# A fused RWKV and token-mixing kernel: V used as it is loaded, on 64-row tiles, instead of being brought into another order

## The chip, the cores and the metric

The kernel runs on one core of a Trainium2 chip. TensorE (PE) does the matrix products, VectorE (DVE), ScalarE (ACT) and GpSimd (POOL) the elementwise work, and SyncE (SP) issues most of the DMAs. The metric is the device time of one execution in microseconds (us); lower is better. Where the text says "the span", it means the time from the first to the last instruction in the one execution that the hardware profiler recorded.

## The reference

Two layers follow each other. The first is a recurrence over 768 time steps, for 4 batches and 8 heads with 48 values each; the second mixes the tokens of a batch.

```python
for t in range(S):                                   # S = 768
    cur = np.einsum('bhd,bhe->bhde', u[None] * kt, vt)
    y[:, :, t] = np.einsum('bhd,bhde->bhe', rt, state + cur)
    state = wt[:, :, :, None] * state + np.einsum('bhd,bhe->bhde', kt, vt)
...
x = y.transpose(0, 2, 1, 3).reshape(B, S, H * D)     # H * D = 384
wq, wk = x @ w_q, x @ w_k                            # d_hyper = 64
W_tok = scale * np.einsum('bsd,btd->bst', wq, wk)
mixed = np.einsum('bst,btd->bsd', W_tok, x)
out = np.maximum(mixed, 0.0) @ w_out
```

`w` is a decay between 0.8 and 0.95, and `u` is a bonus that only the present step's key and value get. Inputs and output are float32.

## The kernel before

The recurrence is computed in chunks of 128 steps. Two chunks make a *unit*; a batch has three units and the kernel twelve. For a unit, four loads bring w, k, r and v (384 KB each). One partition of a load holds two neighbouring time steps of all heads, so that a row in DRAM is 384 bytes long; partitions 0 to 63 then hold the first chunk and 64 to 127 the second. The steps of a unit, by the names that the profile shows, are these:

- `lw`: logarithm of w (ACT). `cw`: its running sum by a product with a triangular matrix CM, whose columns bring the even and the odd time steps apart. `ep` and `en`: exp of plus and minus that sum (ACT).
- `kT`, `rT`: k and r (cast to bfloat16 as `k16`, `r16`) are transposed on PE; `ks` is a copy of k transposed, `qT` the product of r and k. `RT` is r times `ep`, `KT` is k times `en`.
- `A`: KT against RT, the scores of a chunk, two heads at a time on the two halves of the array's rows; `AM`: the scores under the causal mask US (DVE, L713).
- `v16`, `vp`, `VB`: v is cast, brought by PE into the even-then-odd order that all else has (`vp`, by a permutation matrix PM or by identity blocks), and copied out of PSUM. In the last batch the two loads `vw` bring V in that order directly, with 64 partitions and 192-byte rows each.
- `dps`, `dd`: the bonus per head and step; `Vd`: VB times that bonus (POOL, L693).
- `kb`, `kd`: KT transposed back; `sn`, `SB`: the new state, from kd and VB, plus the old state through the scaled identity IDU, times the decay (DVE, L772).
- `yi`, `ya`: old state times RT, and AM times VB, added in PSUM. `X` is that sum times a factor per time step (`gx`) plus Vd, in one DVE instruction (scalar_tensor_tensor, L831). The decay is shifted by an amount that grows with the time step, and gx, gv and gk take it out again.
- `xt`, `XT`: X transposed. `qk`, `QK`: the products with w_q (twice side by side, 128 columns) and w_k, and their copy.

When a batch's three units are done, `T` adds up K times X over the six chunks (two halves of PSUM's partitions get the even and the odd chunks), `mx` multiplies with Q, `MX` is the relu, `fp` the product with w_out, `os` its copy out of PSUM and `st` the store. In the last unit most steps are done chunk by chunk.

PE addresses its array as one tile of 128 rows by 128 columns, or as two of 64 by 128, or two of 128 by 64, or four of 64 by 64. Tiles that differ run side by side. In the profile's rows "128\*128", "64\*128", "48\*128" (48 rows of a 64-row tile), "128\*64" and "64\*64" stand for that. Every matmul is recorded in the helper `mm`, so all have one line, L275.

The order of the work is written out: a `Plan` holds every step, with the engines that may do it, and the lists RANK (the place of each step on its engine) and ALT (which engine or which form it takes) fix one order. `Plan.order` only merges the engines' lists. Buffers are rings (`RINGS`: four for each load, four for `os`), and PSUM's eight banks are handed out in the plan's order. Loads and stores are all on SP's queue but for two: a load waits there until its ring has a free buffer, and everything behind it waits too. `Z` products are fillers without a use in the result.

Of the kernel before, what the change touches and what calls it, by code (L numbers as in the profile page):

```python
# [10 lines left out]
F32 = mybir.dt.float32  # L11
# [22 lines left out]
class Plan:  # L34
# [15 lines left out]
    def add(self, key, engs, fn, after=(), buf=None, reads=(), lag=None, mode=0, behind=None,  # L50
            part=None):
        opts = {}
        for e, x in engs.items():
            x = x if isinstance(x, tuple) else (x, mode, None)
            own = self.AFTER[e.upper()] if lag is None else lag
            over = self.OVER.get(e, 0) if fn is not None else 0
            opts[e] = (e.upper(), x[0] - over, own + over, x[1], x[2])
# [135 lines left out]
    0, 0, 0, 0, 2, 7, 4, 3, 5, 6, 17, 0, 0, 18, 3, 1, 4, 2, 0, 0, 0, 1, 0, 0, 2, 0, 0, 4, 0, 0,  # L193
    1, 2, 1, 4, 3, 4, 3, 6, 5, 5, 8, 8, 13, 10, 9, 12, 11, 5, 17, 9, 26, 19, 9, 11, 18, 15, 22,
    16, 12, 14, 16, 8, 23, 18, 30, 22, 42, 44, 43, 45, 30, 74, 27, 87, 34, 3, 0, 0, 5, 0, 0, 6,
    0, 0, 7, 0, 0, 7, 6, 7, 21, 10, 11, 24, 25, 17, 23, 21, 20, 8, 27, 13, 37, 17, 14, 41, 27,
    32, 24, 31, 15, 38, 26, 56, 32, 52, 55, 64, 68, 37, 82, 32, 90, 36, 9, 0, 0, 8, 0, 0, 11, 0,
    0, 10, 0, 0, 14, 12, 12, 35, 18, 16, 36, 46, 25, 28, 29, 13, 10, 47, 20, 62, 34, 15, 53, 31,
    59, 33, 54, 21, 63, 35, 69, 71, 73, 72, 39, 84, 35, 92, 38, 98, 41, 103, 43, 110, 47, 49, 0,
    0, 115, 49, 127, 55, 50, 0, 0, 126, 68, 139, 60, 51, 0, 0, 12, 0, 0, 14, 0, 0, 15, 0, 0, 16,  # L200
    0, 0, 19, 22, 17, 60, 24, 25, 66, 76, 36, 41, 40, 38, 16, 78, 29, 81, 31, 20, 80, 43, 86,
    46, 79, 42, 83, 44, 96, 50, 89, 95, 91, 97, 51, 106, 44, 124, 52, 13, 0, 0, 18, 0, 0, 19, 0,
    0, 22, 0, 0, 23, 30, 33, 70, 26, 28, 85, 88, 45, 47, 48, 19, 21, 100, 42, 108, 57, 26, 104,
    54, 93, 49, 99, 52, 107, 58, 113, 60, 118, 120, 123, 122, 66, 141, 61, 154, 67, 21, 0, 0,
    20, 0, 0, 23, 0, 0, 24, 0, 0, 37, 22, 23, 94, 40, 39, 101, 105, 53, 56, 55, 25, 24, 109, 46,
    111, 59, 29, 116, 62, 114, 61, 112, 48, 125, 65, 128, 129, 131, 133, 70, 146, 64, 160, 70,
    170, 75, 174, 78, 186, 83, 48, 0, 0, 177, 79, 209, 98, 52, 0, 0, 189, 86, 219, 101, 53, 0,
# [28 lines left out]
def kernel(  # L236
# [63 lines left out]
    if not WHOLE:  # L300
        del RINGS["vw"]
# [726 lines left out]
```

## Time and profile before

| | |
|---|---|
| time, median of 3 runs | 105.08 us (104.53, 105.49, 105.08) |
| span of the profiled execution | 101.6 us; the page gives no other time of it, so 3.5 us of the median lie around the span |
| granted PE clock | 0.992 over the span (0.85 from 95 us on, 1.00 before) |
| PE busy | 90.9 us, 1,881 matmuls and as many weight loads |
| DVE, ACT, POOL busy | 84.2, 80.6 and 64.9 us |
| DMA | 24.66 MB, mean 243 GB/s; queue q1 takes 87.3% of 16 engines |
| last load issued, landed | 70.9 us, 75.8 us |
| last product `fp` | from 94.2 to 97.3 us; the last store is issued at 97.8 and has landed by 100.4 |

A matmul's row gives the time from its start to a modelled end, some 180 to 330 ns, while the next matmul starts much earlier. How long a step holds PE is therefore read from the start of its first matmul to the start of the next step's.

### The profile page before, as it was taken

Reading aid. Unit: us, or ns where it says so; the run is one execution under the profiler, and the core shown is the slowest. Engines: PE = TensorE matmul, PEld = TensorE weight load, DVE = VectorE, ACT = ScalarE, POOL = GpSimd, SP = SyncE. Lnnn points to the kernel's source line nnn. Section 1 sums busy time; section 2 is a strip of 40 time slices with the busy share of each in tenths; the row PEclk is TensorE's granted clock in tenths of the full one; section 3 lists DMA queues with packets and bytes.
Section 4 is the critical chain, followed back from the end, with each engine's and each line's share of the span. In section 5 each row is a group of like instructions: output and inputs, shape, how many; then the busy total and the mean of one; then the engine's idle time right before and its main releaser. Section 6 shows DMA issues by size and latency. Waiting matters only on the chain.

```text
span 101.6 us, 4422 instructions
## 1 busy us (share of the span) xinstructions
PE 90.9 (90%) x1881; PEld 65.5 (64%) x1881; DVE 84.2 (83%) x146; ACT 80.6 (79%) x123; POOL 64.9 (64%) x75
## 2 busy tenths in 40 slices
PE   5968897999989989999899999998999999999920
PEld 2344674757748766677586985776888677967600
DVE  5089998799889969979999999999989999894500
ACT  6364697959699789998999999999987946666940
POOL 6474662991895699889968999896899540000000
PEclk9999999999999999999999999999999999999996
DMA  1999999999999999999999799999999132103793
GB/s 38 310 324 325 325 321 248 296 308 259 321 275 274 304 248 305 300 320 240 275 302 279 198 256 286 167 196 186 211 371 350 39 155 105 56 3 155 284 365 125
DMA packets 56403, 24.66 MB, mean 243 GB/s; under 512 B 54080, under 2 KB 55232, under 8 KB 56384
## 3 DMA queue, kind: packets, MB, share of 16 engines
q1 hardware_dynamic: 56224, 24.19, 87.3%
q8 instruction: 14, 0.23, 0.9%
q10 hardware_dynamic: 160, 0.20, 0.5%
q14 instruction: 5, 0.04, 0.1%
HBM read 19.66 MB, written 4.72 MB: 240 GB/s over the span
## 4 chain that ended last, share of the span: by engine, by line
PE 57%; DVE 10%; SPq 9%; ACT 7%; DMA 6%; POOL 3%; issue 3%; DVEq 0%; ACTq 0%; POOLq 0%
PE PS L275 57%; SPq L328 9%; DMA wg<-in_w_dram 6%; DVE AM L713 5%; ACT lw L500 2%; POOL Vd L693 1%; DVE ks L426 1%; DVE qT L599 1%; ACT os L420 1%; POOL r L511 1%; ACT QK L420 1%; ACT ep L551 1%; DVE X L831 1%; DVE SB L772 1%; ACT XT L420 1%
## 5 line engine op out<-in xcount | busy, mean ns | idle before, releaser
L713 DVE TENSOR_TENSOR AM<-PS,US 128x1024 bf16<-128x1024 f32 x24 | 28.9, 1218 | 0.8 <-PE PS L275 0.8
L693 POOL TENSOR_TENSOR Vd<-VB,dd 128x768 bf16<-128x768 bf16 (+1 forms) x14 | 18.3, 1316 | 5.0 <-DVE dd L426 3.8
L624 POOL TENSOR_TENSOR KT<-ks,en 128x1024 bf16<-128x1024 bf16 x8 | 17.1, 2132 | 5.1 <-DVE ks L426 4.8
L551 ACT ACTIVATE ep<-PS 128x1024 bf16<-128x1024 f32 (+1 forms) x14 | 12.9, 927 | 1.3 <-PE PS L275 0.8
L275 PE MATMUL PS<-wo,MX 128*128 128x384 bf16 x72 | 13.3, 326 | 0.2 <-DVE SB L772 0.2
L556 ACT ACTIVATE en<-PS 128x1024 bf16<-128x1024 f32 (+1 forms) x14 | 12.5, 903 | 0.9 <-PE PS L275 0.9
L275 PEld LDWEIGHTS <-KT 48*128 48x128 bf16 (+1 forms) x304 | 10.0, 94 | 4.7 <-issue 2.7
L275 PE MATMUL PS<-Z 128*128 128x512 bf16 x36 | 11.9, 435 | 1.0 <-DVE Z L342 1.0
L831 DVE SCALAR_TENSOR_TENSOR X<-PS,gx,Vd 128x768 bf16<-128x768 f32 (+1 forms) x13 | 12.4, 950 | 0.3 <-PE PS L275 0.2
L500 ACT ACTIVATE lw<-wg 128x768 bf16<-128x768 f32 x12 | 10.2, 849 | 2.6 <-DMA wg<-in_w_dram 2.6
L420 ACT COPY os<-PS 128x768 f32<-128x768 f32 (+1 forms) x14 | 9.3, 663 | 2.7 <-PE PS L275 2.6
L511 POOL CAST r<-rg 128x768 bf16<-128x768 f32 x11 | 9.6, 872 | 0.4 <-DMA rg<-in_r_dram 0.4
L275 PE MATMUL PS<-RT,KT 48*128 48x128 bf16 x192 | 9.6, 218 | 0.0
L647 POOL CAST v<-vg 128x768 bf16<-128x768 f32 x9 | 7.4, 825 | 3.5 <-DMA vg<-in_v_dram 3.5
L275 PEld LDWEIGHTS <-MX 128*128 128x128 bf16 x72 | 6.5, 97 | 4.3 <-issue 0.9
L420 ACT COPY XT<-PS 128x768 bf16<-128x768 bf16 (+1 forms) x11 | 8.5, 771 | 0.5 <-ACT en L556 0.2
L614 DVE TENSOR_TENSOR RT<-PS,ep 128x1024 bf16<-128x1024 bf16 (+1 forms) x14 | 8.4, 606 | 0.3 <-PE PS L275 0.3
L599 DVE TENSOR_TENSOR qT<-PS,ks 128x1024 bf16<-128x1024 bf16 x12 | 8.2, 683 | 0.4 <-PE PS L275 0.4
L275 PE MATMUL PS<-SB,RT 48*128 48x48 bf16 x160 | 6.7, 182 | 1.9 <-ACT QK L420 0.2
L772 DVE TENSOR_TENSOR SB<-PS,ep 128x192 bf16<-128x192 f32 x20 | 7.0, 351 | 1.4 <-PE PS L275 1.4
L275 PE MATMUL PS<-CM,lw 64*128 64x128 bf16 x192 | 7.5, 217 | 0.8 <-ACT lw L500 0.8
L275 PE MATMUL PS<-VB,AM 128*128 128x48 bf16 x192 | 8.2, 184 | 0.0
(89 smaller groups left out, 192.4 us busy)
## 6 DMA issues: line engine op xcount, KB each, us to landing
wg<-in_w_dram SPq DMA_DIRECT2D x12, 384.0 KB, 5.1
kg<-in_k_dram SPq DMA_DIRECT2D x12, 384.0 KB, 5.5
rg<-in_r_dram SPq DMA_DIRECT2D x12, 384.0 KB, 5.6
vg<-in_v_dram SPq DMA_DIRECT2D x9, 384.0 KB, 5.6
out_dram<-os SPq DMA_DIRECT2D x9, 384.0 KB, 2.4
vw<-in_v_dram SPq DMA_DIRECT2D x4, 288.0 KB, 6.6
out_dram<-os SPq DMA_DIRECT2D x5, 192.0 KB, 2.4
wof<-in_moe_w_out_dram SPq DMA_DIRECT2D x1, 576.0 KB, 4.9
```

Of the source, the lines that this page charges most:

```text
L275: return nc.tensor.matmul(o, l, rr, start=start, stop=stop, skip_group_check=True, is_transpose=trans)
L328: nc.sync.dma_start(out=view(tl, 0, [[D2, H], [1, D2]]), in_=ap[b, :, ds(i * U, U)].rearrange("h (p j) d -> p h (j d)", j=2))
L420: nc.scalar.copy(o, i)
L500: nc.scalar.activation(view(lw.tile, 0, [[64, H], [512, 2], [1, D]]), view(g["wg"].tile, 0, [[D2, H], [D, 2], [1, D]]), ACT.Ln, bias=0.0, ...
L511: op(view(o.tile, 0, [[64, H], [512, 2], [1, D]]), view(g[src].tile, 0, [[D2, H], [D, 2], [1, D]]))
L551: nc.scalar.activation(view(ep.tile, cs[0] * NP * EW + 66, [[EW, NP * len(cs)], [-65, 2], [1, 64]]), at(cw)[:, ds(cs[0] * 512, w_)], ACT.E ...
L556: nc.scalar.activation(en.tile[:, ds(cs[0] * 512, w_)], at(cw)[:, ds(cs[0] * 512, w_)], ACT.Exp, bias=0.0, scale=-1.0)
L599: lambda e: nc.vector.tensor_tensor(view(qT.tile, 0, [[512, 2], [1, 512]]), turned(second), view(ks.tile, 0, [[512, 2], [1, 512]]), ALU.mult),
L624: x.tensor_tensor(o, view(ks.tile, cs[0] * 512, dims), y, ALU.mult)
L693: nc.gpsimd.tensor_tensor(Vd.tile[:, cols], VB.tile[:, cols], view(dd.tile, cs[0] * H, [[1, len(cs) * H], [0, D]]), ALU.mult)
L713: AMs[c] = add(("AM", n, c), {"D": 1221}, lambda e, c=c, A=A: nc.vector.tensor_tensor(view(AM[c].tile, 0, [[C, 8], [1, C]]), view(at(A), 0 ...
L831: nc.vector.scalar_tensor_tensor(view(X.tile, (2 * i + c0) * DM, [[DM, nc_], [1, DM]]), view(at(y), 0, [[512, nc_], [1, DM]]), gx, view(Vd ...
```

## The change

V stays in the order in which it was loaded: partitions 0 to 63 hold the first chunk, two neighbouring time steps side by side (index j). Whatever meets V is turned to suit it.

- `vp`, `VB`, PM and the `vw` loads go; the last batch loads V like the others (12 `vg` loads of 128 partitions).
- `A` is cut by j instead of by chunk: its outputs are 64 partitions (one chunk's even or odd keys). `ya` contracts over 64 rows, for two chunks, two j and two halves of the output: 64 matmuls per unit on 64x64 tiles where there were 16. `kb` and `sn` are cut alike; the old state is added by `so`, two matmuls of 128x64 per chunk.
- `Vd` is v16 times the bonus; it is added in PSUM by four products with identity blocks (`yd`), and `X` becomes a plain copy that ACT or DVE can do.
- The decay's shift is one constant (`up`, `dn` as biases of `ep` and `en`); gx, gv and gk go, and US is a 128x256 mask without factors, made on POOL.
- Q is computed once, chunk 0 on partitions 0 to 63 and chunk 1 on 64 to 127; QK has 256 columns where it had 384. `T` adds all six chunks on both halves (12 matmuls where there were 6), and `mx` takes 64 rows per chunk.
- `cw`, `kT`, `rT`, `xt`, `mx` and `fp` may be cut in two halves of output partitions (`mms`), which puts them on 64x64 or 128x64 tiles.
- `os` has 7 buffers (4 before), `v16` 3 (2 before); RANK and ALT are new.

The counts, from the two programs' instruction lists: PE has 3,941 matmuls (1,881 before), 3,000 of them on 64x64 tiles (12 before). The tile shape changes 103 times along PE's list (99 before). Z products are 22 (36 before). PE's queue drains go from 16 to 3. Leaving out waits, branches, table loads and DMAs, DVE has 144 instructions (146 before), ACT 111 (122) and POOL 65 (75). SP starts with k, w, r, k, v, w, r, w where it started with w, k, r, w, v, k, r, v, k, w; one store of 384 KB stands ahead of the last four loads, where all stores stood behind all loads.

```diff
+    def mms(split, o, l, rr, **kw):
+        if not split:
+            return mm(o, l, rr, **kw)
+        for half in range(2):
+            mm(o[ds(half * 64, 64)], l[:, ds(half * 64, 64)], rr, **kw)
...
-        wg=(4, HW, F32), rg=(4, HW, F32), kg=(4, HW, F32), vg=(4, HW, F32), os=(4, 2 * DM, F32),
...
+        wg=(4, HW, F32), rg=(4, HW, F32), kg=(4, HW, F32), vg=(4, HW, F32), os=(7, 2 * DM, F32),
...
-                vps = add(("vp", n), {"E": (330, 1, None), "e": (185, 3, None)}, f_vp,
-                          [v16s, wts["p"]], vp, [v16])
-                VBs = add(("VB", n), copies(2 * DM), lambda e: copy(
-                    e, view(VB.tile, 0, [[DM, 2], [1, DM]]),
-                    view(at(vp), 0, [[512, 2], [1, DM]])), [vps], VB, [vp])
...
+        Vds = add(("Vd", n), {"P": 1477, "D": 900}, lambda e: (
+            nc.vector if e == "D" else nc.gpsimd).tensor_tensor(
+            Vd.tile, v16.tile, view(dd.tile, 0, [[1, 2 * H], [0, D]]), ALU.mult),
+            [v16s, dds], Vd, [v16, dd])
...
-                        mm(x[:, ds(hh * 512 + hp * C, C)],
-                           KT.tile[ds(hh * 64, D), ds((c * NP + hp) * C, C)],
-                           RT.tile[ds(hh * 64, D), ds((c * NP + hp) * C, C)])
+                    for c in range(2):
+                        for hh in range(2):
+                            x = (c * NP + hp) * C
+                            mm(at(A)[ds(c * 64, 64), ds(hh * 512 + hp * C, C)],
+                               KT.tile[ds(hh * 64, D), ds(x + j * 64, 64)],
+                               RT.tile[ds(hh * 64, D), ds(x, C)])
...
-                        mm(x[:, ds(hp * D, D)],
-                           kd.tile[:, ds(64 + (c * H + h) * 128 - 64 * hh, 128)],
-                           VB.tile[:, ds(c * DM + h * D, D)],
...
+                            mm(at(sn)[ds(hh * 64, 64), ds(c * 512 + hp * D, D)],
+                               kd.tile[rows, ds(hh * 512 + (j * NP + hp) * 64, 64)],
+                               v16.tile[rows, ds(j * DM + (2 * hp + hh) * D, D)],
+                               start=(j == 0 and hp == 0))
...
-                if not first:
-                    nc.tensor.drain()
                 for hp in range(NP):
                     for c, hh in side:
-                        mm(of(c, 2 * hp + hh), RT.tile[ds(hh * 64, D), ds((c * NP + hp) * C, C)],
+                        mms(first, of(c, 2 * hp + hh),
+                            RT.tile[ds(hh * 64, D), ds((c * NP + hp) * C, C)],
...
-                    mm(of(c, h), AM[c].tile[:, ds(hh * 512 + hp * C, C)],
-                       VB.tile[:, ds(c * DM + h * D, D)],
+                    for c in range(2):
+                        rows = ds(c * 64, 64)
+                        mms(True, of(c, h), AM[j].tile[rows, ds(hh * 512 + hp * C, C)],
+                            v16.tile[rows, ds(j * DM + h * D, D)],
...
+        def f_yd(e):
+            for j in range(2):
+                for c in range(2):
+                    rows = ds(c * 64, 64)
+                    mm(of(c, 0, H)[ds(j * 64, 64)], ID16[rows, rows], Vd.tile[rows, ds(j * DM, DM)],
+                       start=False)
...
-                nc.vector.scalar_tensor_tensor(
-                    view(X.tile, (2 * i + c0) * DM, [[DM, nc_], [1, DM]]),
-                    view(at(y), 0, [[512, nc_], [1, DM]]), gx,
-                    view(Vd.tile, c0 * DM, [[DM, nc_], [1, DM]]), ALU.mult, ALU.add)
+            xs = add(("X", n, c0), copies(DM * nc_), lambda e, c0=c0, nc_=nc_: copy(
+                e, view(X.tile, (2 * i + c0) * DM, [[DM, nc_], [1, DM]]),
+                view(at(y), c0 * 512, [[512, nc_], [1, DM]])),
+                [*yas, yds, *yis[1]], X, [y], part=c0 if end else None)
...
+                        for half in range(2):
+                            mm(x[ds(half * 64, 64), ds(128 + c * DH, DH)],
+                               XT.tile[:, ds(kt * nq + k_ * C + half * 64, 64)],
+                               wk_sb[:, ds(kt * DH, DH)], start=(kt == 0 and k_ == 0),
...
+                        mm(x[ds(c * 64, 64), ds(0, C)], wq_sb[:, ds(kt * DH, DH)],
+                           XT.tile[:, ds(kt * nq + k_ * C, C)], start=False,
...
-                mm(at(T)[ds(c * DH, DH), ds(0, DM)], QK.tile[:, ds(ii * QS + U + c * DH, DH)],
-                   X.tile[:, ds(gi * DM, DM)], start=(gi < 2), stop=(gi >= NCH - 2))
+                for half in range(2):
+                    mm(at(T)[ds(half * DH, DH), ds(0, DM)],
+                       QK.tile[:, ds(ii * QS + 128 + c * DH, DH)],
+                       X.tile[:, ds(gi * DM, DM)], start=(gi == 0), stop=(gi == NCH - 1))
```

## The prediction

> **What bounds the kernel now.** First the page's busy shares and its forty slices, then the chain that ended last, then the busy time of each engine by stage.
>
> ```profile
> PE 90.9 (90%) x1881; PEld 65.5 (64%) x1881; DVE 84.2 (83%) x146; ACT 80.6 (79%) x123; POOL 64.9 (64%) x75
> ...
> PE   5968897999989989999899999998999999999920
> ...
> DVE  5089998799889969979999999999989999894500
> ...
> DMA  1999999999999999999999799999999132103793
> ...
> PE 57%; DVE 10%; SPq 9%; ACT 7%; DMA 6%; POOL 3%; issue 3%; DVEq 0%; ACTq 0%; POOLq 0%
> ```
>
> ```profile
> 50.00:60.00 10.00, 9.74 (x254) 7.90 (x255) 9.96 (x15) 9.83 (x15) 8.82 (x9) 1.00 0.98 259
> 60.00:70.00 10.00, 9.38 (x274) 7.03 (x268) 9.77 (x15) 9.81 (x15) 9.71 (x9) 1.00 1.09 220
> ...
> 90.00:95.00 5.00, 5.00 (x55) 3.45 (x54) 3.31 (x7) 3.44 (x9) 0.00 (x0) 1.00 0.39 155
> ```
>
> The stage rows give the length, then busy us of PE, PEld, DVE, ACT, POOL, the granted clock (1.00), DMA share and GB/s. From 50 to 70 us every engine is full and the DMA queues too; after the last load (75.8 us) POOL and DVE run dry, and PE alone stays full until 97.3. PE has 57% of the chain, so its work is the first sum; that of DVE, ACT and POOL decides how long PE waits.
>
> **How long a matmul holds PE.** PE's timeline, start against start:
>
> ```profile
> 57.60 0.37 PE L275 MATMUL PS<-VB,AM 128*128 128x48 bf16 x8
> 57.81 0.61 PE L275 MATMUL PS<-ID,KT 128*128 128x128 bf16 x8
> ...
> 60.02 0.40 PE L275 MATMUL PS<-ID,k 64*128 64x64 bf16 x16
> 60.26 0.40 PE L275 MATMUL PS<-ID,r 64*128 64x64 bf16 x16
> 60.59 0.26 PE L275 MATMUL PS<-SB,IDU 128*128 128x192 bf16 x1
> ```
>
> ```profile
> 42.18 0.36 PE L275 MATMUL PS<-v,ID 64*64 64x384 bf16 x4
> 42.48 1.14 PE L275 MATMUL PS<-wo,MX 128*128 128x384 bf16 x6
> ```
>
> Eight small products on the whole array take 0.21 us, 26 ns each. Sixteen on two row tiles take 0.24, 15 each (13 where only 48 columns stream): a tile needs 26 to 29 ns for a pair of load and matmul, and the two tiles overlap. The second sixteen take 0.33, because the shape changes behind them: 95 ns per change. Four 384-column products on four tiles pass in 0.30 with a change, some 50 each, against 162 each on the whole array: four tiles stream side by side.
>
> **PE's sum.** The trace has no row for many small matmuls on 64x64 tiles, 2,176 of the new list. Bounds: no row shows a tile faster than 26 ns a pair, so 6.5 each; if cutting columns gains nothing, 13 each as on two tiles. Between them I go by the weight loads:
>
> ```profile
> L275 PEld LDWEIGHTS <-AM 128*128 128x128 bf16 x192 | 6.5, 96 | 0.8 <-issue 0.2
> ...
> L275 PEld LDWEIGHTS <-QK 128*64 128x64 bf16 x24 | 1.0, 109 | 0.4
> ...
> L275 PEld LDWEIGHTS <-ID 64*64 64x64 bf16 x12 | 0.3, 103 | 0.3
> ```
>
> A column-cut load lasts 7 to 13 ns longer than a full one (96). So 26 + 7 = 33 ns a pair: 8.3 each on four tiles, 16.5 on two (336 of 128x64). Products of 128, 192 and 384 columns go by columns: 27 and 13.4 for 128 on two and four tiles, 42 for 192 on two, 81 and 40 for 384. By step, us before and after:
>
> - order of V 2.4 (24x80 + 12x40) to 0; bonus `yd` 0 to 1.9 (48x40)
> - `ya` 5.0 (192x26) to 6.4 (768x8.3)
> - `sn` and old state 5.5 (160x26 + 16x88) to 4.0 (320x8.3 + 32x42)
> - `kb` 3.6 to 2.7; `kT`, `rT` 6.6 to 6.9; `xt` 3.7 to 3.2; `dps` 2.5 (96x26) to 3.2 (192x16.5)
> - `yi` 3.1 (160x13, and 13 drains, each of some 0.08 by PE's idle time behind them) to 2.4
> - `qk` 6.0 (72x29 + 33x110 + 6x56) to 4.3 (144x16.5 + 72x27); `T` 1.9 to 3.8 (48x80); `mx` 4.0 to 2.1
> - `cw` 5.2, `A` 5.1 and `fp` 11.7 stay: these are bound by columns.
>
> Together 66.3 to 62.8. With 99 and 103 changes of shape at 0.095 (9.4 and 9.8): 75.7 to 72.6, **3.1 less**. At 6.5 and 13 for the pairs another 5.1 goes.
>
> The Trainium skill, "TensorEngine Tiling (Array Packing)", Restrictions, says that column tiling switches the fast weight load off, which speaks against this change. The rows of 103 and 109 ns agree in sign, not in size; by the rule the sum would be that of the second rival.
>
> **The other engines**, by their rows in the groups by shape:
>
> - DVE: `X` loses 11x1.01 and 2x0.61 and keeps two copies (1.5): -10.8; zeroing of kd and US -1.9; MX -2.1; against that copies from ACT: os +3.0, XT +2.2, QK +1.1, and Vd, ks, KT, TS, a cast, together +3. Sum -5.5 of 84.2. The Vd on DVE has no row; 0.7 (a bfloat16 product of 1024) to 1.5 (POOL's), I take 0.9.
> - ACT: VB -7.2 (9x0.80), X +8.5, XT -3.2, os -2.6, casts -0.9, QK -2, MX +1.8, kd +1.5: -5.8 of 80.6 with the rest. The bias of exp I cost at nothing, between a gain of its two 0.2 us set-up rows and 0.05 each.
> - POOL: VB -2.5 (3x0.83), Vd -2.2, one KT fewer -2.1, casts +2.5, PM, iota and wq -1.9: -5.6 of 64.9 with the rest. The mask moved to POOL (four selects, 0.29 each) is beside the first loads; with that cover gone it is 1.2.
>
> So each does 6 to 9% less. **DMA**: three loads of 384 KB stand for four of 288; bytes are equal, rows 3,072 fewer of the page's 56,224 packets in q1, at its mean of 25 ns on 16 engines at most 4.8 us of transfer. That lies beside full engines: 0 on the path, to 3 where the last unit would wait. **SP**: k comes first, so the first logarithm starts one load (1.2 us) later, beside fillers; the third unit's w comes two places earlier, and the chain waits for just that load (issued at 10.15, landed at 16.2): 0 to 2.4 gained; I take 0, since PE works through older units meanwhile. One store now has four loads behind it; with 7 `os` buffers its copy should be done long before (in the trace the first was at 43.8).
>
> **Sum.** From 10 to 97.3 us PE has 87.3. About 2.0 of its 75.7 was done by 10, so 73.7 is work, 18 fillers take 3.9 (216 ns each), and 9.7 it waits: 13.6 without use. After: 70.6 of work, and 7% less waiting, because the engines waited for do 7% less: 12.6. 83.2 instead of 87.3: **4.1 less**. The profiled span of 101.6 becomes 97.5; with the 3.5 around it as in the median of the runs, 105.08 becomes **101.0 us**.
>
> **Rivals.**
>
> 1. *Four tiles run as fast as two, tile by tile* (26 ns a pair): 5.1 less again, 95.9. For it: the two-tile rows show no loss by overlap. Against it: the longer loads.
> 2. *Column-cut weights load slowly.* If 64 columns cost a tile twice the pair's 26 ns, the 2,176 take 12.75 each (+9.7) and the 336 take 25.5 (+3.0): 101.0 + 12.7 = 113.7, or 107.5 if PE's waiting absorbs half of its 12.6. It decides from about 41 ns a pair, where 2,176 x 2 ns eat the 4.1. Against it: loads only 7 to 13 ns longer.
> 3. *PE runs out of instructions*, which ends slower. The page shows a queue that fetches them:
>
> ```profile
> q8 instruction: 14, 0.23, 0.9%
> ```
>
> 14 packets for some 3,785 instructions, about one per 256, each 0.9% x 16 x 101.6 / 14 = 1.0 us on a DMA engine. The changed list has 7,892: 31 blocks. By the prices above a block ran at least 3.7 us, and will run 1.3 to 5.8; 15 of 31 run under 2. If a block is asked for only when the one before it starts, and is there 2 us later, PE waits 4.8 in all (105.8); at 2.2 it is 7.9 (108.9), at 2.5 14.0 (115). It decides from 2 us. For it: the packets come one per block. Against it: nothing in this trace shows PE starved; how far ahead it fetches cannot be read here.
>
> The Trainium skill, "Runtime: NRT & Kernel Launch", Instruction fetch mechanics, gives PE a store of 2,048 instructions in blocks of 256, by which nothing would be lost; the same section also speaks of two blocks only.
>
> 4. *PE's gain is waited away.* A unit's chain is longer: both chunks' KT and RT before either `A`, and Vd, `yd`, then `X`. If waiting grows by 4 us the time stays at 105.
>
> **How the numbers follow.** Forecast (99 to 104) 0.43; rival 1 0.17; rival 4 and its like, within 1%, 0.13; rival 2 0.10; rival 3 0.17. Faster by over 1% (about what a measurement of this kernel can tell) 0.60, same 0.13, slower 0.27. The range reaches from rival 1's 95.9 to 110, into rivals 2 and 3, and leaves out their far ends.
>
> **What would show it.** Steps of 32 small matmuls on 64x64 tiles 0.26 to 0.28 us from start to start (0.21: rival 1; 0.41: rival 2); gaps inside such steps with no releaser, one per 128 pairs, near the fetch packets (rival 3); DVE near 79, ACT 75, POOL 59; PE's share of the chain at 55% or more. More idle time of PE behind AM, X or Vd speaks for rival 4. The prediction is wrong if four tiles do not share the array as two do.

## The result and the profile after

The changed kernel takes **149.87 us** (median of 4 runs, 147.29 to 152.05). The kernel before, run beside it, takes 105.27 (104.53 to 105.49): 1.407 times as long, with a 95% interval from 1.394 to 1.421. Executions of one kernel differ by some per cent in time and granted clock, so the ratios here go by the fast ones alone (147.29 and 148.41 us of the changed kernel, with a clock of 0.80 and 0.78), while its profile is of the slowest, 152.05 us with a span of 150.0 and a clock of 0.73. The forecast was 101.0 us, in a range from 95.9 to 110. Both the sign and the range are wrong.

The page of the changed kernel, the lines that answer to those shown of before:

```profile
PE 113.5 (76%) x3941; PEld 85.1 (57%) x3941; DVE 83.0 (55%) x144; ACT 79.0 (53%) x112; POOL 58.9 (39%) x65
...
PE   7589687566983859985859917999685798779970
...
DVE  3288855414751635878425726479574468723740
...
PEclk9959855555555555799655995569999559986996
DMA  4999999979989998857700990000002002620465
...
q8 instruction: 31, 0.51, 1.4%
...
PE 70%; issue 20%; DMA 3%; DVE 2%; SPq 1%; ACT 1%; DVEq 0%
```

Four things are new. No engine is full any more, where before all four were near 90% in the middle of the span. The granted clock (PEclk) is at 5 tenths in 18 of 40 slices; before it was 1.00 up to 95 us. The chain that ended last has 20% "issue", time in which the engine waited for nothing that the profile shows, where it had 3%. And there are 31 packets of instructions where there were 14.

The same stretches as before, and a late one (length, then busy us of PE, PEld, DVE, ACT and POOL, granted clock, DMA share, GB/s):

```profile
50.00:60.00 10.00, 7.88 (x268) 6.55 (x264) 4.87 (x8) 4.75 (x7) 0.57 (x1) 0.50 1.01 268
60.00:70.00 10.00, 8.22 (x410) 6.84 (x405) 7.84 (x14) 5.99 (x10) 8.42 (x9) 0.89 0.67 169
90.00:95.00 5.00, 4.08 (x145) 3.15 (x144) 2.87 (x4) 2.47 (x4) 2.57 (x3) 0.50 0.05 12
```

From 50 to 60 us PE starts as many matmuls as before (268 against 254), but it has more than twice as many to start. DVE and ACT do half of what they did there, since they wait for PE. The waits say for what PE waits in its turn (us in total, times, longest us):

```profile
PEld L274 <- issue: 45.8, 72, 3.2
...
PE PS L274 <- issue: 28.3, 21, 3.0
```

Before, the first of these was far smaller, and the second was not among the longest waits:

```profile
PEld L275 <- issue: 13.4, 51, 0.4
```

Such a wait of 3 us stands in the middle of a step, between two products of the same kind. PE's timeline (start, length, what, and in brackets the idle time before it):

```profile
86.48 0.38 PE L274 MATMUL PS<-v,AM 64*64 64x48 bf16 x21
89.90 0.26 PE L274 MATMUL PS<-v,AM 64*64 64x48 bf16 x5 [3.04 <-issue]
```

The products belong to one step `ya`; between two of them PE does nothing for 3 us, and the profile names nothing that it waits for.

**Where the gaps stand.** If all of PE's records (weight loads, matmuls and its few waits and drains) are numbered by their start, from 0, the waits stand at fixed numbers: 449, 705, 961, 1217 and so on, one every 256. A block here is the 256 records from one such number to the next, and the gap at its end goes from the start of its last record to the start of the next block; gaps under 0.2 us are left out. Of 30 such block ends 22 have a gap of 0.3 to 3.3 us, and the gaps add up to **33.5 us** (before: one of 0.3). Five blocks of the changed kernel, worked out in this way:

```
first record of block   starts   until the next block starts   gap at its end
             961         25.9            5.37 us                   3.26
            4289         84.6            5.31                      3.23
            5569        105.1            3.45                      1.36
            5825        108.5            3.45                      0.89
            6081        112.0            4.00                      2.02
```

Where two blocks in a row end in a gap, the next one never starts sooner than 3.45 us after the one before it. Over all 30 blocks the mean is 4.41 us. Blocks with a gap at both ends take 3.73 to 5.92 us up to 92 us, when the last load has landed; after that they take 3.45 to 4.0, and one beside stores 4.83. After a gap PE goes on 1.3 to 1.5 us after the end of a packet on q8. So a block's time has three parts, by the packets' times in the trace: at 105.1 us the packet starts 1.05 us after the block, takes 0.92, and the next block starts 1.48 after its end, together 3.45; at 31.3 us, beside loads, these are 3.58, 1.02 and 1.32, together 5.92. The blocks of before followed each other by 4.8 us and more, so the same limit would hardly show there.

**The clock.** From the matmuls' shapes one can add up how long columns streamed in PE (columns / 2.4 per ns at full clock, as in m1 below, where 384 columns take 164 ns; twice that at half; divided by the number of tiles that run side by side), in windows of 3.41 us, since the steps of the granted clock lie whole multiples of that apart. In the traces of the two kernels and of the first four experiments, each of 28 falls of the clock follows a window whose share was 0.34 or less, and none one of 0.37 or more. The bounds are not sharp: three windows of 0.30 to 0.33 were not followed by a fall (the changed kernel's from 65.6 us is one), and the clock came back after windows of 0.72 and more, while several of 0.70 to 0.72 left it at half. The kernel before has 0.5 to 0.98 in all windows up to its end. In the profiled execution of the changed kernel the clock is half for 81 of 150 us: a window with a 2 us gap, filled with products of 48 columns, falls short. The Trainium skill, "TensorE: Matmul & The Clock Gate", What's actually happening, has the clock go to half after an idle window of 3413 ns; the length agrees with the trace, but the windows here were up to a third full.

### The profile page after: what moved, and what is told of

Same layout as the page of the kernel before. It is cut to its first block, busy times and chain, and to the rows that moved or that the text cites. A ratio compares the mean times of both kernels' runs of the same rounds, so it can differ in the third digit from the quotient of the medians.

```text
span 150.0 us, 8494 instructions
## 1 busy us (share of the span) xinstructions
PE 113.5 (76%) x3941; PEld 85.1 (57%) x3941; DVE 83.0 (55%) x144; ACT 79.0 (53%) x112; POOL 58.9 (39%) x65
## 4 chain that ended last, share of the span: by engine, by line
PE 70%; issue 20%; DMA 3%; DVE 2%; SPq 1%; ACT 1%; DVEq 0%
PE PS L274 70%; DMA rg<-in_r_dram 3%; DVE AM L651 1%; SPq L327 1%; ACT os L402 1%; DVE r L481 0%; DVE kd L410 0%; DVE SB L706 0%; DVE k L493 0%; DVE r L362 0%; DVE k L362 0%; DVE lw L362 0%; DVE IDU L421 0%; DVEq L706 0%
## 5 line engine op out<-in xcount | busy, mean ns | idle before, releaser
L651 DVE TENSOR_TENSOR AM<-PS,US 128x1024 bf16<-128x1024 f32 x24 | 29.1, 1221 | 14.8 <-PE PS L274 14.5
L632 POOL TENSOR_TENSOR Vd<-v,dd 128x768 bf16<-128x768 bf16 x11 | 16.3, 1478 | 32.9 <-ACT dd L402 17.1
L596 POOL TENSOR_TENSOR KT<-ks,en 128x1024 bf16<-128x1024 bf16 x7 | 14.9, 2123 | 28.7 <-DVE ks L408 24.8
L274 PE MATMUL PS<-v,AM 64*64 64x48 bf16 x768 | 13.6, 208 | 11.0 <-issue 11.0
L274 PEld LDWEIGHTS <-AM 64*64 64x64 bf16 x768 | 11.5, 130 | 12.0 <-issue 11.6
L274 PEld LDWEIGHTS <-KT 48*64 48x64 bf16 x704 | 13.2, 130 | 8.9 <-issue 8.5
L274 PE MATMUL PS<-RT,KT 48*64 48x128 bf16 x384 | 13.7, 256 | 4.8 <-issue 4.3
L528 ACT ACTIVATE en<-PS,dn 128x1024 bf16<-128x1024 f32 (+1 forms) x14 | 13.7, 993 | 6.4 <-PE PS L274 6.4
L274 PE MATMUL PS<-wo,MX 128*64 128x384 bf16 (+1 forms) x108 | 16.4, 382 | 0.0
L522 ACT ACTIVATE ep<-PS,up 128x1024 bf16<-128x1024 f32 (+1 forms) x14 | 13.9, 1010 | 1.9 <-PE PS L274 1.9
L470 ACT ACTIVATE lw<-wg 128x768 bf16<-128x768 f32 x12 | 10.1, 842 | 4.2 <-DMA wg<-in_w_dram 4.2
L274 PE MATMUL PS<-CM,lw 64*64 64x128 bf16 (+1 forms) x352 | 10.2, 259 | 1.0 <-ACT lw L470 1.0
L274 PE MATMUL PS<-SB,RT 48*64 48x48 bf16 (+1 forms) x240 | 8.8, 207 | 2.6 <-issue 2.6
```

The costliest lines, as they stand in the source:

```text
L274: return nc.tensor.matmul(o, l, rr, start=start, stop=stop, skip_group_check=True, is_transpose=trans)
L470: nc.scalar.activation(view(lw.tile, 0, [[64, H], [512, 2], [1, D]]), view(g["wg"].tile, 0, [[D2, H], [D, 2], [1, D]]), ACT.Ln, bias=0.0, ...
L522: nc.scalar.activation(view(ep.tile, cs[0] * NP * EW + RS, [[EW, n4], [1 - RS, 2], [1, R]]), view(at(cw), cs[0] * 512, [[C, n4], [R, 2], [ ...
L528: nc.scalar.activation(en.tile[:, ds(cs[0] * 512, w_)], at(cw)[:, ds(cs[0] * 512, w_)], ACT.Exp, bias=dn, scale=-1.0)
L596: x.tensor_tensor(KT.tile[:, w], ks.tile[:, w], en.tile[:, w], ALU.mult)
L632: nc.vector if e == "D" else nc.gpsimd).tensor_tensor(
```

## The experiments

### Cutting matmuls of the kernel before, joining those of the changed one

If the number of instructions is the cause, the kernel before must become as slow when its matmuls are cut and nothing else is changed, and the changed kernel must become faster when cuts are taken back. In e1 nearly every product with 128 output partitions becomes two with 64 (3,657 matmuls for 1,881; same order, same loads, nothing changed on the other engines):

```diff
     def mm(o, l, rr, start=True, stop=True, trans=False):
+        if l.shape[-1] == 128 and l.shape[0] >= 48 and len(o.shape) == 2 and l.shape[0] <= 128 \
+                and o.shape[0] == 128 and o.shape[-1] < 512:
+            for half in range(2):
+                nc.tensor.matmul(o[ds(half * 64, 64)], l[:, ds(half * 64, 64)], rr, start=start,
...
+            return
```

> The kernel before, with nearly every matmul of 128 output partitions cut into two of 64, one after the other: 3,657 matmuls instead of 1,881, the same columns streamed, the same order of steps, 100 changes of shape instead of 99; V, bonus, mask, DVE, ACT, POOL and DMA work are untouched. Theory 1 (PE is short of instructions: a block of 256 is not had in less than 3.5 us, 3.7 to 5.9 while loads run): 28.7 blocks instead of 14.8, none of which has 3.5 us of work any more, so 125 to 145 us, with gaps of 0.5 to 3 us exactly every 256 instructions, and DVE, ACT and POOL as busy as before. Theory 2 (small tiles are slow in themselves: a 64-column weight load costs a tile 51 ns): some 21 us more, 126, but spread evenly over the matmuls, without such gaps. Theory 3 (the other changes, V's order, the longer chain of a unit, the new order of steps, cost the time): 103 to 107.

Measured: **144.63 us** (142.18 to 145.16) against 104.89 for the kernel before. The gaps at block ends are 26.0 us, the mean block 4.38 us. Page of this kernel, busy shares and the chain that ended last:

```profile
PE 110.0 (78%) x3657; PEld 82.7 (59%) x3657; DVE 87.1 (62%) x146; ACT 82.3 (59%) x123; POOL 64.9 (46%) x75
...
PEclk9999999997555899999599599999559999999997
...
PE 66%; issue 18%; SPq 6%; DMA 4%; ACT 2%; DVE 1%; ACTq 0%; DVEq 0%
```

It is the picture of the changed kernel, made out of the old one: V's new way, the bonus in PSUM, the constant shift and the new order have no part in it, so none of them is needed for it. The span is 38.9 us longer than before; 26.0 are gaps at block ends, and 10.1 us of columns (at full clock) streamed at half clock.

In e2 the optional cuts of the changed kernel are taken back (`cw`, `kT`, `rT`, `mx`, `fp` and `xt` on the whole array or two tiles: 3,405 matmuls, 136 changes of shape for 103):

```diff
         e = e if e in opts else next(iter(opts))
+        if e == "f" or (e == "e" and key[0] in ("cw", "kT", "rT", "mx", "fp")):
+            e = {"f": "e", "e": "E"}[e]
```

> The changed kernel, with the optional cuts taken back (cw, kT, rT, mx, fp whole where the plan had them halved, xt on two tiles instead of four): 3,405 matmuls instead of 3,941, and 136 changes of shape instead of 103. Theory 1 (short of instructions): 4.2 blocks fewer at some 4.4 us each, so 18 us less, 125 to 138. Theory 2 (64x64 tiles slow at 51 ns a load): 2,000 instead of 3,000 on 64x64, less too, some 5 us less one way and 3 more for the changes of shape: 143 to 150. Theory 3 (order and chain): 149 to 155, since it does 3 us more of changes of shape and nothing else moves.

Measured: **137.54 us** (137.37 to 141.99), ratio to the kernel before 1.313 (1.308 to 1.318); gaps at block ends 17.4 us. In e3 `ya` is joined as well (two products of 64x128 tiles where there were four of 64x64, and a drain before and after: 3,021 matmuls, 150 changes of shape):

```diff
             def f_ya(e, j=j):
+                nc.tensor.drain()
...
-                        mms(True, of(c, h), AM[j].tile[rows, ds(hh * 512 + hp * C, C)],
+                        mms(False, of(c, h), AM[j].tile[rows, ds(hh * 512 + hp * C, C)],
...
+                nc.tensor.drain()
```

> As the run before, and ya joined too (AM times V on two tiles of 64 rows, 384 matmuls instead of 768, with a drain of PE before and behind each of its 24 steps): 3,021 matmuls, 150 changes of shape. Theory 1 (short of instructions): 7.2 blocks fewer than the changed kernel, 30 us less, 112 to 128. Theory 3 (order and chain): 155 to 160, for 47 more changes of shape and 48 drains at 0.1 us each.

Measured: **136.73 us** (134.82 to 138.54), ratio 1.306 (1.284 to 1.327). The gaps at block ends have indeed gone down to 8.2 us, but the time hardly went with them, and the expected 112 to 128 are missed. The waits of e2 and of e3 show what took their place:

```profile
PEld L276 <- issue: 32.4, 70, 3.2
...
PE PS L276 <- issue: 14.3, 13, 3.0
```

```profile
PEld L276 <- issue: 34.1, 109, 2.0
...
PE PS L276 <- issue: 6.8, 10, 1.8
```

The first two are of e2, the others of e3. The matmuls' own waits are halved, from 14.3 to 6.8 us. Before the weight loads there is as much waiting as in e2, but in 109 short pieces where there were 70; the added drains and changes of shape (47 more than in the changed kernel) make such pieces. The clock is half for 52 of e3's 133 us, though few blocks end in a gap, and 16.3 us of columns (at full clock) stream in that time. An estimate from these numbers: e3's span is 31.4 us longer than that of the kernel before; 7.9 are gaps, at most 16.3 the half clock, 4.8 the 51 more changes of shape and 2.8 the 35 more drains, at the 0.095 and 0.08 us that the prediction read from the trace of before, together at most 31.8. So the fetch alone does not make the 45 us; what shape changes, drains and the clock each cost in e3 no run separates.

### The dose

In e6 and e7 fewer matmuls of the kernel before are cut: `cw` and `A` in e6, and also `kT`, `rT` and the last `xt` in e7. The edit of e6:

```diff
+        if l.shape[-1] == 128 and l.shape[0] in (48, 64) and o.shape[-1] == 128 and not trans:
+            for half in range(2):
```

> The kernel before with only cw and A cut in two (128 columns each, so the same streaming time): 2,265 matmuls, 17.8 blocks of 256 instructions, 123 changes of shape (24 more, 2.3 us at 0.095). A block then stands for some 4.9 us of the kernel's pace. Theory 1 (a block is had in 3.5 us in quiet, 3.7 to 5 under loads): hardly any waiting, 105 to 109. If each added matmul cost a fixed price, as the 1,776 of the run with nearly all halved cost 22 ns each: 384 x 22 = 8.6, so 113.5.

> The kernel before with cw, A, kT, rT and the last xt cut: 2,609 matmuls, 20.4 blocks, 129 changes of shape. A block stands for 4.3 us of pace, inside what a block takes under loads (3.7 to 5.9). Theory 1: waits in some blocks, 108 to 117. At a fixed price of 22 ns each: 121.

Measured: e6 **108.11 us**, ratio 1.022 (1.012 to 1.032); e7 **119.13**, ratio 1.120 (1.106 to 1.133). e6 lies in the range of theory 1 and 5 us under the fixed price; e7 lies between the two, 2 us over the one and 2 under the other, and decides nothing by itself. By number of matmuls:

| kernel | matmuls | blocks of 256 | time, us | gaps at block ends | us at half clock |
|---|---|---|---|---|---|
| before | 1,881 | 14.8 | 105.3 | 0.3 | 1.6 (at its end) |
| e6 | 2,265 | 17.8 | 108.1 | 5.0 | 0.4 |
| e7 | 2,609 | 20.5 | 119.1 | 9.4 | 12.2 |
| e1 | 3,657 | 28.7 | 144.6 | 26.0 | 28.7 |
| e3 (changed) | 3,021 | 23.8 | 136.7 | 8.2 | 51.8 |
| e2 (changed) | 3,405 | 26.6 | 137.5 | 17.4 | 59.3 |
| changed | 3,941 | 30.8 | 149.9 | 33.5 | 80.9 |

Times are medians; the last two columns are of the profiled execution (152.05 us for the changed kernel, 109.51 for e6). A fixed price per instruction would give a straight line from the first row. The first 384 cuts cost 3 us, the next 344 cost 11. That fits the gaps' column: what counts is how many blocks hold less work than their successor takes to come.

### The fetch by itself

A kernel without the computation streams matmuls of one kind after another, some thousand of each, with all operands in place.

```diff
+        one(512, 40)
+        one(48, 984)
+        four(48, 1024)
...
+        four(384, 512)
```

> Nothing of the computation: long streams of matmuls on constant data, no loads beside them; the stores of zeros come at the end. In order: 40 of 128x128 with 512 columns, 984 of 128x128 with 48, 1,024 of 64x64 with 48, 32 of 512, 992 of 64x64 with 128, 1,024 of 64x128 with 48, 512 of 64x64 with 384, 256 of 128x128 with 256, 512 of 64x64 with 48. Theory 1 (a block of 256 instructions takes at least 3.4 us to come): every stream of short matmuls runs at 27 ns a pair in the mean, whatever its tiles: within a block 6 to 9 ns on four tiles, 13 on two, 26 on one, and a gap of 2 us or more at the end of each block for four tiles, 1.7 for two, next to none for one; the streams of 384 and 256 columns have no gaps. Theory 2 (tiles slow in themselves): four tiles 13 ns a pair throughout, no gaps. Of the clock: if idle time behind the gaps halves it, it is 0.5 in the streams on four and two tiles with 48 columns and 1.0 in those of 384 and 256 columns; if small tiles count as idle, it is 0.5 in the stream of 64x64 with 384 columns too.

Products of 48 columns on four 64x64 tiles, at the step from full to half clock; each line is one block of 128 matmuls:

```profile
44.18 1.23 PE L48 MATMUL PS<-M,W 64*64 64x48 bf16 x128 [1.59 <-issue]
47.63 1.36 PE L48 MATMUL PS<-M,W 64*64 64x48 bf16 x128 [2.23 <-issue]
```

128 of them run in 1.04 us from first to last start at full clock, **8.2 ns each**, and in 1.68 us at half clock (13.3 each). Either way the next block starts only **3.45 to 4.0 us** after this one. That holds for 128 columns too; with 384 columns on the same tiles a block takes 5.2 us, ends in no gap and keeps the clock at 1.00. On the whole array, 48 columns, 128 products take 3.3 us and the block 3.45 to 4.0. A block that follows 11 us of long products passes without a gap and the next one doesn't: what is fetched ahead is about one block. The Trainium skill, "Runtime: NRT & Kernel Launch", Instruction fetch mechanics, gives PE a store of 2,048 instructions; by that the first eight blocks of a stream would pass at once, and the trace disagrees. The two blocks that the same section names are nearer to it.

The second such kernel runs 22 blocks of the same small products while 44 loads of 384 KB and then the stores of zeros run.

```diff
+        one(512, 20)
...
+                    nc.sync.dma_start(
...
+        four(48, 2816)
```

> Nothing of the computation is done; the output is zeros. 2,816 products of 64x64 with 48 columns on four tiles, 22 blocks of 256 instructions, while 44 loads of 384 KB run beside the first some 50 us of them and nothing after. Theory 1 (loads lengthen the fetch of a block): 4.0 to 5.5 us a block while the loads run, 3.45 to 3.75 after; 22 blocks take 85 to 105 us. Rival (the longer blocks of the changed kernel come from its own waits and not from the loads): 3.45 to 3.75 us in every block, 76 to 83 us in all.

```profile
42.92 1.91 PE L48 MATMUL PS<-M,W 64*64 64x48 bf16 x128 [2.64 <-issue]
48.57 1.91 PE L48 MATMUL PS<-M,W 64*64 64x48 bf16 x128 [3.74 <-issue]
...
81.69 1.91 PE L48 MATMUL PS<-M,W 64*64 64x48 bf16 x128 [2.65 <-issue]
85.14 1.91 PE L48 MATMUL PS<-M,W 64*64 64x48 bf16 x128 [1.54 <-issue]
88.59 1.91 PE L48 MATMUL PS<-M,W 64*64 64x48 bf16 x128 [1.55 <-issue]
```

The 16 blocks up to 81.7 us, beside the transfers, take 3.73 to 5.65 us each, 4.46 in the mean; after them 3.45 to 3.73. Nothing but the transfers differs between the two, so it is they that lengthen a block's fetch by about 1 us. By the packets' times, beside transfers a packet of q8 starts 1.8 us after the block and takes 1.3 in the mean, afterwards 1.1 and 1.0: most of the difference is the later start.

### The clock by itself

To tell the share from the gaps, m2 streams products on the whole array with 32, 24, 20 and 16 columns (about 25 ns each, so hardly any gap, and shares from 0.5 down to 0.27), and at the end 80 products of 512 columns on one 64x64 tile alone.

```diff
+        for n, pairs in ((32, 640), (24, 640), (20, 640), (16, 640)):
+            one(512, 48)
+            one(n, pairs)
+        one(512, 48)
+        corner(512, 80)
```

> Nothing of the computation is done; the output is zeros. First six exps of 128x1024 out of PSUM with a constant bias, then six with a bias tile. Then products on the whole array: 48 of 512 columns ahead of each of four streams of 640 products with 32, 24, 20 and 16 columns, at the end 80 products of 512 columns on one 64x64 tile alone, between two groups of 48. Theory 1 (the clock goes by the share of a window of some 3.4 us in which columns stream, and falls under about 0.35): a block of 128 products takes at least 3.45 us, 27 ns a product, so the shares are 0.49, 0.37, 0.31 and 0.25; the clock stays 1.00 with 32 and with 24 columns and falls to 0.5 within 4 to 10 us of the start of 20 and of 16. One tile alone streams all the time and keeps 1.00: 80 products in 17 us. Rival (the clock goes by the stalls at block ends, not by the share): with 27 ns of work a product there are hardly any stalls, and it stays 1.00 in all four streams. Rival (it goes by the part of the array in use): the single tile has a quarter of it, so the clock falls there and 80 products take some 34 us. The bias tile: 1.05 us an exp with a constant and 1.13 with a tile, 85 ns more; if the dearer exp of the changed kernel came from what ran beside it, both are the same within 10 ns.

Stretches of 4 us of m2, with 32 columns (24.00), with 24 (48.00, 52.00), with 20 (76.00) and with the single tile (136.00):

```profile
24.00:28.00 4.00, 3.90 (x157) 3.82 (x153) 0.00 (x0) 0.00 (x0) 0.00 (x0) 1.00 0.03 8
...
48.00:52.00 4.00, 4.00 (x166) 4.00 (x163) 0.00 (x0) 0.00 (x0) 0.00 (x0) 1.00 0.02 4
52.00:56.00 4.00, 3.63 (x134) 3.48 (x131) 0.00 (x0) 0.00 (x0) 0.00 (x0) 0.71 0.01 4
...
76.00:80.00 4.00, 4.00 (x161) 4.00 (x158) 0.00 (x0) 0.00 (x0) 0.00 (x0) 0.69 0.02 4
...
136.00:140.00 4.00, 4.00 (x21) 1.95 (x19) 0.00 (x0) 0.00 (x0) 0.00 (x0) 1.00 0.00 0
```

With 20 columns PE starts a product every 25 ns without any gap, 4.00 of 4.00 us busy, and the clock still falls, after a window of 0.33. So it is the share of streaming columns, not the gap. With 24 columns two windows at 0.40 keep it, and the first in which the fetch slows PE down (118 products, 0.35) loses it; full clock throughout was expected there, and that part missed. The single tile, a quarter of the array, keeps 1.00: what counts is that columns stream, not in how much of the array. (A tile that runs alone counts as one, so its share is near 1.)

Two attempts to lift the share in the changed kernel failed. In e4 94 filler products of 512 columns (their result is not used) stand between the steps of small products, in e5 the same in e3:

```diff
+    def filler(x, m):
+        rows = ds(0, 64) if m == 3 else ds(0, 128)
+        mm(PS[ds(0, 64), ds(x * 512, 512)], Z[rows, ds(0, 64)],
...
+        if m == 3:
+            nc.tensor.drain()
```

> The changed kernel with 94 more products that nobody reads (zeros, 512 columns on one tile of the shape in force, 216 ns at full clock, into a PSUM bank that is free at that place of the plan). They do no work, and stand for the fillers that the changed kernel has fewer of. In the traces so far the clock fell to half behind every 3.4 us window in which columns streamed for less than 0.35 of the time, and came back behind one of 0.72 and more. Theory 1a (the clock is a part of the loss, and comes from too little streaming): the granted clock goes from 0.72 to 0.80 to 0.88 or more, and the time falls by 3 to 12 us, to 138 to 147, though there are 188 instructions more. Theory 1b (the block's 3.5 us is all, the clock costs nothing): 151 to 156.

> The same 94 or so fillers in the changed kernel with the optional cuts taken back and ya joined (3,021 matmuls, 136.7 us, where the gaps at the block ends came to only 8 us and the clock was 0.81). Theory 1a (clock): 0.9 or more and 120 to 131 us. Theory 1b (instructions only): 137 to 143.

Measured: **179.33 us** (ratio 1.700, 1.677 to 1.722) and **175.86**, far above what either theory gave. The group of the added products in e4:

```profile
L289 PE MATMUL PS<-Z 64*64 64x512 bf16 x60 | 27.2, 453 | 2.5 <-issue 2.5
L289 PE MATMUL PS<-Z 128*64 128x512 bf16 x34 | 15.2, 453 | 0.0
```

They take 42 us on PE beside the work that it had, with a drain behind 60 of them; the granted clock is 0.80, no higher than in two of the changed kernel's four executions, and still half for 72 us. PE has most of the chain, so it fits that whatever is put on it to keep the clock has to be paid there. These runs say nothing of what the clock alone costs.

The other direction says more. The kernel before has 18 fillers after 10 us. In e8 17 of them are left out, in e10 the last 7, in e11 the last 11:

```diff
             s_["rank"] = x
+            if s_["key"][0] == "z" and x >= 28:
+                s_["way"], s_["dur"] = "e", 0
```

> The kernel before without the 17 filler products that stand behind the first 10 us (216 ns each, 3.7 us; nothing else changes place). By the trace of before, the share of each 3.4 us window in which columns stream is 0.55 to 0.71 from 11 to 30 us with them, and 0.40 to 0.60 without. Theory 1 (the clock falls only where the share goes under about 0.35): the clock stays 1.00 and the time is 102 to 105.2 us, up to 3.7 less if PE was the path there and unchanged if the fillers stood in waits. Rival (a lower bound, such as 0.5, holds the clock in the kernel itself): half clock in two to six windows between 11 and 30 us and 106 to 112 us.

> The kernel before without the last 7 fillers (from 23 us on, 1.5 us). By the shares of before, no window goes under 0.42 without them. Theory 1 (17 fillers less gave nothing because the half clock of 14 us took back what their own 3.7 us gave): the clock stays 1.00 and the time is 0.5 to 1.5 us under the kernel before, 102.8 to 104.8. Rival (the fillers stand in waits, and the half clock cost nothing there): within 0.4 us of the kernel before.

> The kernel before without the last 11 fillers (from 21 us on, 2.4 us). By the shares of before the lowest window is 0.39 without them, just over the 0.35 at which the clock fell elsewhere. Theory 1: where the clock stays 1.00, 1 to 2.4 us under the kernel before, 102 to 104.3; where one window goes under 0.35 it is half for some 7 us or more, and the gain is gone. Rival (fillers in waits): within 0.4 us of the kernel before.

Measured, as ratios to the kernel before: e8 1.002 (0.997 to 1.007), e10 1.000 (0.994 to 1.006), e11 0.994 (0.988 to 1.001). In the profiled execution of e8 the clock is lost for 14 us:

```profile
PE   6968972997998998999899999998999999999940
...
PEclk9999999555558999999999999999999999999997
```

The window from 15.0 us has a share of 0.26, where 0.40 had been estimated for it: the estimate fell, the bound of 0.35 held again, and the clock came back only after a window of 0.79. Its other executions have granted clocks of 0.925 to 0.967 (0.929 in this one), so some lost the clock for about half as long. With 3.7 us of fillers less and up to 14 us of half clock more the time is the same; e10 fits fillers that stand in waits anyway, and e11, in which the clock also fell once for 3.4 us (share 0.34 where 0.39 had been estimated), has at most 1.2% to gain. e8 and e11 differ by 0.8 us, give or take 0.9, so what the half clock costs in that stretch is not resolved. That PE has waits there that absorb it would explain why it is little, but this is argued only. No version beats the kernel before beyond the uncertainty.

### The order of the loads

The only other part of the change tried alone is the order of the first loads (k first, the third unit's w two places earlier), in the kernel before:

```diff
+        first = [("kg", 0), ("wg", 0), ("rg", 0), ("kg", 1), ("vg", 0), ("wg", 1), ("rg", 1), ("wg", 2),
+                 ("vg", 1), ("kg", 2)]
```

> The kernel before with the first ten loads in the changed kernel's order (k first; the third unit's w two places earlier); PE's list is as it was. The prediction took 0 for this between a gain of 2.4 and a loss of one load (1.2 us) at the first logarithm. That step: 104 to 105.6 us. If the wait for the third unit's w was on the path: 102.5 to 104. If the first logarithm's delay is: 105.8 to 106.8.

Measured: 105.34 us, ratio 1.012 (1.004 to 1.021). It costs 0.4 to 2.2 us in that kernel. The middle, 1.3 us, is about the one load by which the first logarithm starts later (5.5 us where it was 4.2, in the traces); that this delay is the cause was not tried by itself.

## Why the prediction was wrong

**The step that failed is the sum's: PE's time was made of its own work, and the fetch stood in it as a rival with a small chance and too small a size.** Rival 3 named the mechanism, the place (once per 128 pairs) and what would show it, all of which came: e1 and m1 show it. It got a chance of 0.17, and a block of 2 to 2.5 us counted from the start of the one before, worked out from nothing but the 1.0 us that a packet takes. Measured are 3.45 us at the least, 4.46 in the mean under loads (m3) and 4.41 over the changed kernel's 30 blocks. Those 30 are 132 us; with 11.7 before them and 6 behind, that is the span of 150. "How far ahead it fetches cannot be read here" and "nothing in this trace shows PE starved" were too quick. By the packets' times in the trace of before, in 13 of its 14 blocks the packet of q8 ends 2.0 to 3.5 us after the block's start, and the shortest block (4.76 us) ends in a gap of 0.31 us, after which PE goes on 1.5 us after the packet's end. That makes 3.5 to 5.0 us a block, where the rival had 2 to 2.5. Even without the packets' times the trace of before left more open than the rival took: no block of it was followed in under 4.8 us, so anything between the packet's 1.0 and 4.8 was possible, and 15 of the 31 new blocks were to hold under 2. At the upper end 30 blocks alone are over 140 us, and no row excluded it.

**The clock was in no step.** The prediction priced everything at full clock. In the profiled execution of the changed kernel half the span runs at half, and the columns that stream in it, 24.1 us at full clock, take twice that. How much of this is on the path is not settled: 12.3 of the 24.1 us lie in blocks that end in a gap, where m1's blocks take the same 3.45 to 4.0 us at either clock; 10.2 lie in blocks without a gap (the rest is before the first block or behind the last). An estimate of the span's 48.4 us more is then 33.5 us of gaps, 10.2 to 24.1 of clock, less the 4.1 expected to be saved: between 39.6 and 53.5. The lower value takes it that all of the clock's loss in blocks without a gap is on the path, which no run shows. That both are there is shown by e1 and m2; how they divide the 48.4 stays open.

**Steps that held:**

- *8.3 ns for a small matmul on four tiles.* m1 has 8.2. In the changed kernel a step of 32 at full clock passes in 0.27 us, as forecast (0.26 to 0.28); PE's timeline:

```profile
108.69 0.45 PE L274 MATMUL PS<-ID,k 64*64 64x64 bf16 x32
108.96 0.40 PE L274 MATMUL PS<-RT,KT 48*64 48x128 bf16 x16
```

- With that, rivals 1 (6.5) and 2 (12.75) fall. The rule of the Trainium skill, "TensorEngine Tiling (Array Packing)", Restrictions, that column tiling switches the fast weight load off, shows a small price here: a tile needs 33 ns a pair, against 25 on the whole array in the same run, far from the 51 of rival 2.
- *POOL* lost 6.0 us of busy time (5.6 forecast), `Vd` on DVE took 0.95 us (0.9 forecast, 0.7 to 1.5), and X, XT, QK, os and MX on DVE and ACT changed by what was forecast, within 0.2 us each.

**Sizes that were off:** DVE lost 1.2 us of busy time and ACT 1.6, where 5.5 and 5.8 were forecast. The durations added up fall by 4.2 and 4.3 us, but they overlap less: by 8.2 us on DVE and 7.8 on ACT before (sum less busy time), by 5.2 and 5.1 after, which fits engines that wait for PE between operations. On ACT the exp's bias is the mis-sized term. It was costed at nothing; the changed kernel has 1132 and 1114 ns for `ep` and `en` where the kernel before had 1048 and 1024, and m2 shows that it is the operand, with a bias tile (first line) and a constant:

```profile
L82 ACT ACTIVATE E<-PS,ZB 128x1024 bf16<-128x1024 f32 x6 | 6.7, 1114 | 0.2
L80 ACT ACTIVATE E<-PS 128x1024 bf16<-128x1024 f32 x6 | 6.1, 1023 | 2.2 <-DVE PS L78 2.0
```

91 ns each; 28 of them are 2.5 us. The Trainium skill, "ScalarE: Activation LUTs", What ACT_TABLE_LOAD costs, gives about 93 ns for each such operand; the run agrees, and the prediction should have used it. The *load order*, taken as 0 from a range of 0 to 2.4 gained, cost 0.4 to 2.2 us in e9: by its size, the term that was named and set to nothing, the first logarithm's delay by a load, outweighed the gain there. The *store ahead of the last four loads*, which the prediction expected to hold nothing up, was issued only at 81.8 us, 12 us after the load before it, and the last loads landed at 91.6 us, where they had landed by 75.8. The chain that ended last waits for none of them: its only wait for a load lies in the first 7 us.

Rival 4 (PE's gain waited away) can't be told apart in the changed kernel, where the other engines wait for a PE that itself waits for its instructions.

## What to carry to other kernels

Count PE's instructions, not only its work. In runs of short work a block of 256 (128 loads and 128 matmuls) was not followed in under 3.45 us here, and in 4.5 in the mean while loads ran, so a matmul costs some 27 to 35 ns of the span whatever its tile; cutting one into halves that run side by side gains nothing where that fills the blocks with short products. And look at how much of each 3.4 us columns stream: where it was under about 0.35 the clock halved here with few exceptions, and it came back only after more than 0.7.

## What the runs showed of the hardware

- PE takes its instructions in blocks of 256; with blocks of short work they follow each other by 3.45 to 4.0 us, and by 3.73 to 5.65 us (mean 4.46) beside transfers of 250 to 320 GB/s (m1, m3). The next block starts 1.2 to 1.6 us after its packet on q8 ends, with few exceptions.
- Four 64x64 tiles take a load and matmul of 48 columns every 8.2 ns at full clock and every 13.3 at half (m1); half clock adds just the columns' 20 ns to a tile's 33.
- The clock fell after windows of 3.41 us with a share of 0.35 or less and stayed at 0.37 or more, with one tile or with four; a few windows of 0.30 to 0.33 did not bring it down. It came back after 0.72 to 0.79 and more, and not after 0.63 in m2 or 0.75 in e8.
- A single 64x64 tile that streams all the time keeps the full clock (m2).
